# The small row transfers of a decode step's gradients: from ScalarE's queue inside wo's backward pass to SP's queue behind its last load

## The chip, the cores and the metric

The kernel runs on one core of one Trainium2 chip. The metric is device time in microseconds (us). A profiled execution has a span, which runs from its first to its last instruction, and a time, which also holds what lies around the span. The engines are named as in the profile: PE (TensorE matmuls), PEld (its weight loads), DVE (VectorE), ACT (ScalarE), POOL (GpSimd) and SP (SyncE, which here only issues transfers). PEq, ACTq and SPq are the sequencers of these engines, which issue transfers and wait on semaphores.

## What is computed

Four layers are run on one token (attention A, dense block B, A, B, with the same weights for both A and both B), and then the gradients of all weights, of both caches and of the input:

```python
def _A_ref(x, k_cache, v_cache, wq, wo):          # 32 query heads, 4 kv heads, window of 4096
    q = (x @ wq).reshape(B, Sq, Hq, Dh).transpose(0, 2, 1, 3)
    k = jnp.repeat(k_cache[:, :, Sk - W:, :], rep, axis=1)
    v = jnp.repeat(v_cache[:, :, Sk - W:, :], rep, axis=1)
    p = _softmax(jnp.einsum("bhqd,bhkd->bhqk", q, k) * (Dh ** -0.5), axis=-1)
    o = jnp.einsum("bhqk,bhkd->bhqd", p, v)
    return o.transpose(0, 2, 1, 3).reshape(B, Sq, Hq * Dh) @ wo
def _B_ref(x, w1, b1, w2):                        # mish: h * tanh(softplus(h))
    h = jnp.einsum("bsd,df->bsf", x, w1) + b1
    ...
    return jnp.einsum("bsf,fd->bsd", act, w2)
x = x + _A_ref(_layernorm(x), ...); x = x + _B_ref(_layernorm(x), ...)   # twice
_out, _vjp = jax.vjp(_f, A_x, A_k_cache, A_v_cache, A_wq, A_wo, B_w1, B_b1, B_w2)
```

With one token, the gradient of a weight matrix is a sum of two outer products, one for each use of the weight: out_4 (wq), out_5 (wo), out_6 (w1) and out_8 (w2). The caches hold 32768 positions, of which only the last 4096 have a gradient; the rest of out_2 and out_3 is written with zeros.

## The kernel before

**Weights come through a ring.** `Ring` hands out slots of 1 MB in SBUF. A load is issued on SP's queue (L71) when a slot is free; `release` frees a slot, and the next load in the list goes out when the products that read the slot are done. The last loads of the kernel are the eight chunks of wo for the backward pass of the first attention layer (key `("o", 3)`) and four chunks of wq (key `("q", 3)`, chunks 0 to 3; chunks 4 to 7 are still in the ring). They are called wo 0 to wo 7 and wq 0 to wq 3 here. A release is put off by some products (`later`), so that wq 0 goes out when wo 1 is used up, and wq 3 when wo 4 is.

**Zeros fill the memory's time.** `zeros(n)` issues n transfers of 1 MB of zeros on POOL's queue (L265). Where it is given a tile, the tile's being written holds the transfers back, so that they start at a chosen point of the calculation.

**The stage around the change** is the call of `attn_bwd(0, ...)`, from 282 us of the span on. Its first loop is wo's pass: for each of the eight chunks, PE turns blocks of 128x128 (L474) into three PSUM buffers named BIG, ACT and DVE copy them back (L309, L306), and PE multiplies them with the incoming gradient (L493); from chunk 2 on DVE takes a quarter of the chunk as a dot of rows (L451). After each chunk the function `do1` runs. Then follow the scores' gradient (L922 to L929), `dp1`, the query's gradient (L938, L940), `dq1`, and wq's pass, a loop over eight chunks with `dn1` after each.

**Rows for the gradients.** The outer products need their factors as rows, in two partitions of the tile `ROWS` (a part of W1's storage) at base 0 (out_4), 32 (out_5), 64 (out_6) and 96 (out_8). Three functions put them there by small transfers on ACT's queue:

- `rowize` turns GA, GB or DQC on PE (L1010), copies the result on ACT (L1013) and issues two transfers (L1015).
- `take_back` brings AC, NB, OC and NA back from DRAM (L819), where the forward pass had put them.
- `rowize_f` turns DHC on PE, copies it on ACT into the tile `rf` (L859) and issues two transfers (L861).

In the kernel before, `do1` calls `rowize` for GA and GB after chunk 0, `take_back` four times after chunk 1, and `rowize_f` after chunk 2. After chunk 5 it issues two transfers of zeros and sends out_0 and out_7 on ACT's queue (`store_rows`, L326; `store_f`, L871, by way of `rf` too). `dq1` calls `rowize` for DQC.

**Use of the rows.** `dp1` issues four transfers of zeros without a condition, and then calls `work(4)`: four units of outer products (L1051), which PE takes from four lists in turn. A list holds out_8 and out_6 from the start, and out_5 from `do1`'s chunk 3 on. `twins` (L1043, in `dn1` at t = 4, on SP's queue) copies all rows once more for the units after the passes, which take two matmuls side by side. From there on everything is units, their copies out of PSUM, and stores on SP's queue (L1025, L1030).

**Order of waits.** Each engine runs its instructions in the order in which the program writes them, with semaphores between engines. The transfers of SP and ACT take eight completion semaphores in turn, in program order; a transfer waits, before it is issued, for the one eight places ahead of it, whichever of the two queues that is in.

Of the kernel before, what the change touches and what calls it, by code (L numbers as in the profile page):

```python
# [15 lines left out]
P = 128  # L16
HQ = 32
# [3 lines left out]
F = 3584  # L21
G = 4
W = 4096
TD = D // P
# [69 lines left out]
def kernel(  # L94
# [22 lines left out]
    nc = tc.nc  # L117
# [13 lines left out]
    def sb(shape, dtype, name):  # L131
        return keep.tile(shape, dtype, name=name)
# [3 lines left out]
    def tmp(shape, dtype, name):  # L136

        if name not in scratch:
            scratch[name] = keep.tile(shape, dtype, name=name)
        return scratch[name]  # L140
# [31 lines left out]
    def big():  # L172
        if wide:
            wide.append(wide.pop(0))
            return wide[-1][:, 0:512]
        b = bigs[big_n[0] % len(bigs)]
        big_n[0] += 1
        return b
# [16 lines left out]
    for hi in range(4):  # L195
        r = slice(32 * hi, 32 * hi + 32)
# [4 lines left out]
    NA = sb([P, TD, 2], BF16, "NA")  # L201
    NB = sb([P, TD, 2], BF16, "NB")
    GA = sb([P, TD, 2], BF16, "GA")
    GB = sb([P, TD, 2], BF16, "GB")
    OC = sb([P, HQ, 2], BF16, "OC")
    DQC = sb([P, HQ, 2], BF16, "DQC")
    AC = sb([P, TF, 2], BF16, "AC")
# [49 lines left out]
    def zeros(n, after=None):  # L257

        if after is not None and zjobs:
            nc.gpsimd.tensor_copy(pz[0:1, pz_n[0] % 16:pz_n[0] % 16 + 1], after[0:1, 0:1])  # L260
            pz_n[0] += 1
        for _ in range(n):
            if zjobs:
                dst = zjobs.pop()
                nc.gpsimd.dma_start(dst, zt[:])  # L265
# [52 lines left out]
    def store_rows(col_bf, n, out_flat):  # L318

        b = big().bitcast(BF16)  # L320
        nc.tensor.transpose(b[0:n, 0:P], col_bf, ident_bf[:])
        k = so_n[0]
        so_n[0] += 1
        r = rt[0:n, 2 + k, :]
        nc.scalar.copy(r, b[0:n, 0:P])
        nc.scalar.dma_start(out_flat.rearrange("(t p) -> t p", p=P), r)  # L326
# [31 lines left out]
    def to_eight(bank, buf):  # L358

        nc.vector.transpose(buf[:, 0:256], bank[:, 0:256])  # L360
        return buf[:, 0:256].rearrange("p (g m) -> p g m", m=32)[:, :, 0]
# [454 lines left out]

    def take_back(name, base, off):
        r = DR[name][:].rearrange("(n l) p -> l n p", l=2)
        nc.scalar.dma_start(ROWS[base:base + 2, off:off + r.shape[1] * P].rearrange("l (n p) -> l n p", p=P), r)  # L819

    x3, st3, sA1 = attn_fwd(1, x2, st2, False, wo_hook1, last_da)
    put_by("OC", OC, HQ)
# [29 lines left out]
    def rowize_f():  # L852

        b = big().bitcast(BF16)
        for l in range(2):
            for k in range(4):
                nc.tensor.transpose(b[0:7, (4 * l + k) * P:(4 * l + k + 1) * P],
                                    DHC[:, :, l].rearrange("p (c k) -> p k c", k=4)[:, k], ident_bf[:])
        nc.scalar.copy(rf.rearrange("c (l p k) -> c l p k", l=2, k=4), b[0:7].rearrange("c (l k p) -> c l p k", l=2, k=4))  # L859
        for l in range(2):  # L860
            nc.scalar.dma_start(ROWS[64 + l:65 + l, NOFF:NOFF + F].rearrange("o (c j) -> o c j", j=512),  # L861
                              rf[:, 512 * l:512 * l + 512])

    def store_f(col):

        b = big().bitcast(BF16)
        for k in range(4):
            nc.tensor.transpose(b[0:7, k * P:(k + 1) * P], col[:].rearrange("p (c k) -> p k c", k=4)[:, k], ident_bf[:])
        r = rf[:, 0:512]
        nc.scalar.copy(r.rearrange("c (p k) -> c p k", k=4), b[0:7, 0:512].rearrange("c (k p) -> c p k", k=4))  # L870
        nc.scalar.dma_start(out_7.rearrange("(c j) -> c j", j=512), r)  # L871
# [122 lines left out]
    ROWS = W1S[:, 0:5120]  # L994
    NOFF = 1024
# [11 lines left out]
    def rowize(cols, n, base, off):  # L1007

        b = big().bitcast(BF16)
        nc.tensor.transpose(b[0:2 * n, 0:P], cols[:].rearrange("p n l -> p (n l)"), ident_bf[:])  # L1010
        k = rt_n[0]
        rt_n[0] += 1
        nc.scalar.copy(rt[0:2 * n, k, :], b[0:2 * n, 0:P])  # L1013
        for l in range(2):
            nc.scalar.dma_start(ROWS[base + l:base + l + 1, off:off + n * P].rearrange("o (t p) -> o t p", p=P),  # L1015
                              rt[l:2 * n:2, k, :])


    def store(dst, s, old, new, of, last):


        h = (of + 1) // 2
        if new == of:
            lo = sent.pop(id(s), 0)
            nc.sync.dma_start(dst[:, lo * 512:], s[:, lo * 512:of * 512])  # L1025
            stage_free.append(s)
        elif old < h <= new and wide and (last or len(firsts) < 4):
            firsts.append(0)
            sent[id(s)] = new
            nc.sync.dma_start(dst[:, 0:new * 512], s[:, 0:new * 512])  # L1030
# [14 lines left out]
    def unit_dw(base, lo, ro, dst, left):  # L1045


        b, m = rooms(left)
        for i in range(m):
            R, at = ((ROWS, base), (TWIN, base ^ 32))[i]  # L1050
            nc.tensor.matmul(b[:, 512 * i:512 * i + 512], lhsT=R[at:at + 2, lo:lo + P],  # L1051
                             rhs=R[at:at + 2, ro + 512 * i:ro + 512 * i + 512], start=True, stop=True,
                             tile_position=(at, 0))
        evac(dst[:, 0:512 * m], b[:, 0:512 * m], cost=((0.69, 0.585), (1.23, 0.95))[m - 1])
        return m

    def units_rows(base, nblk, out):

        for c in range(nblk // 4):
            s = stage_free.popleft()  # L1060
            for tt in range(4):
                n = 0
                while n < 2:
                    m = unit_dw(base, NOFF + (4 * c + tt) * P, 512 * n, s[:, tt * D + n * 512:(tt + 1) * D], 2 - n)
                    n += m
                    store(out.rearrange("(c p k) d -> p c (k d)", p=P, k=4)[:, c], s, 2 * tt + n - m, 2 * tt + n, 8,
                          c == nblk // 4 - 1)
                    yield
# [41 lines left out]
    todo = [deque() for _ in range(4)]  # L1110
# [47 lines left out]
    do1_acc = tmp([P, HQ], FP32, "da")  # L1158

    def do1(c):  # L1160
        if c == 0:
            rowize(GA, TD, 32, 0)
            rowize(GB, TD, 96, 0)
        if c == 1:
            take_back("AC", 96, NOFF)
            take_back("NB", 64, 0)
            take_back("OC", 32, NOFF)
            take_back("NA", 0, 0)
        if c == 2:
            rowize_f()  # L1170
        if c == 4:
            y = to_eight(YR, RT.rearrange("p a t s -> p (a t s)")[:, 0:512].bitcast(FP32))
            nc.vector.tensor_tensor(out=x4[:], in0=y, in1=x3[:], op=ALU.add)
        if c == 3:
            todo[1].append(units_rows(32, HQ, out_5))
        if c == 5:
            store_rows(x4[:], TD, out_0[0, 0, :])
            store_f(db)
        if c == 5:
            zeros(2, do1_acc[:, 4 * c:4 * c + 1])  # L1180

    def dp1():
        zeros(4)
# [2 lines left out]

    def dq1():
        stage_free.extendleft(KT[:, g].rearrange("p t d -> p (t d)") for g in range(G))
        rowize(DQC, HQ, 0, NOFF)
        zeros(4, DQC[:, 0, 0:1])  # L1190

# [8 lines left out]
    def units_a0(k):  # L1200
# [3 lines left out]
        work(4)  # L1204

    g0 = attn_bwd(0, sA0, g1, ("o", 3), ("q", 3), (), dict(do=do1, dp=dp1, dq=dq1, dn=dn1), units_a0)
    zeros(2, g0)
    g0b = sb([P, TD], BF16, "g0b")
# [48 lines left out]
```

## Time and profile before

| what | value |
|---|---|
| time, median of 3 runs | 456.58 us (456.39 to 457.21) |
| time of the profiled execution | 457.25 us |
| its span | 455.5 us |
| moved by the DMA engines | 181.40 MB, mean 398 GB/s |
| busy share of the span | PE 70%, DVE 58%, ACT 46%, POOL 9% |
| share of the 16 DMA engines' span | q1 (SP's queue) 65.7%, q0 (POOL's, the zeros) 31.2%, q10 (ACT's) 0.1% |

The span is split by the profile into 40 slices of 11.4 us. In its second part a digit is the busy share of a slice in tenths (9 is 90% or more); "GB/s" is what the DMA engines moved in it. A view by windows gives the same for stretches that the reader chooses, and a timeline gives instructions with start, duration, engine, line, operation and tiles, and in brackets the idle time before one and what ended it.

### The profile page before, as it was taken

The page shows a single profiled execution, that of the slowest core. Times are in us where ns is not written, and L with a number is a line of the kernel's source. Part 1 is how long each engine was busy: PE and PEld are TensorE (multiplying, and loading weights), DVE is VectorE, ACT ScalarE, POOL GpSimd, SP SyncE. Part 2 cuts the span into 40 slices and gives each one's busy share as a digit, 9 for nine tenths or more (in the row PEclk, how much of TensorE's full clock was granted, in tenths as well). Part 3 has the DMA queues.
Part 4 walks back from the last instruction along what each step waited for, and adds up shares of the span by engine and source line. Part 5 has one row for each costly group of instructions (what it writes and reads, how often), then busy time and mean ns, then how long its engine had stood idle before and what let it go on. Part 6 is the DMA issues. An engine that isn't in the chain of part 4 may idle for free. (4 is left out here: it accounts for less than half of the span.)

```text
span 455.5 us, 12838 instructions
## 1 busy us (share of the span) xinstructions
PE 318.3 (70%) x5681; PEld 244.4 (54%) x5681; DVE 262.0 (58%) x515; ACT 210.6 (46%) x245; POOL 38.9 (9%) x86
## 2 busy tenths in 40 slices
PE   3835543456699788986898567488896898889900
PEld 3735543445686688976886455487692222234500
DVE  4504746278442764763377447425476999998900
ACT  2501101011067766860384431164166999999900
POOL 1000000002132212102101000003212000000000
PEclk9955555555559899985698757858585555555555
DMA  8999999979999999999999999859999999999997
GB/s 335 422 421 419 418 420 420 419 312 425 395 422 419 422 418 414 398 417 420 424 422 423 423 417 382 328 181 371 419 392 405 408 416 419 415 420 416 406 408 298
DMA packets 28085, 181.40 MB, mean 398 GB/s; under 512 B 3674, under 2 KB 3702, under 8 KB 9462
## 3 DMA queue, kind: packets, MB, share of 16 engines
q1 hardware_dynamic: 19526, 121.76, 65.7%
q0 software_dynamic: 8064, 58.72, 31.2%
q8 instruction: 44, 0.72, 0.6%
q10 hardware_dynamic: 440, 0.10, 0.1%
q14 instruction: 11, 0.09, 0.0%
HBM read 81.84 MB, written 98.62 MB: 396 GB/s over the span
## 5 line engine op out<-in xcount | busy, mean ns | idle before, releaser
L309 ACT COPY ring<-BIG 128x1024 bf16<-128x1024 bf16 x51 | 50.5, 1014 | 56.5 <-PE BIG L474 44.5
L1051 PE MATMUL wide<-W 2*128 2x512 bf16 x228 | 52.1, 598 | 9.3 <-ACT W L309 1.9
L474 PE MATMUL BIG<-ident_bf,ring 128*128 128x128 bf16 x664 | 55.2, 237 | 3.6 <-ACT W L1013 1.6
L474 PEld LDWEIGHTS <-ring 128*128 128x128 bf16 x768 | 52.8, 109 | 5.3 <-issue 4.8
L451 DVE CUSTOM_DVE_ANT_0 junk<-ring,SC 128x1024 bf16<-128x1024 bf16 x32 | 38.9, 1216 | 10.2 <-DMA ring<-in_B_w_dram 9.8
L306 DVE COPY ring<-BIG 128x1024 bf16<-128x1024 bf16 x32 | 21.8, 690 | 28.5 <-PE BIG L474 20.8
L1051 PEld LDWEIGHTS <-W 2*128 2x128 bf16 x240 | 12.5, 102 | 43.9 <-issue 42.8
L493 PEld LDWEIGHTS <-ring 128*128 128x128 bf16 x864 | 30.5, 98 | 10.4 <-issue 6.5
L306 DVE CAST ring<-wide 128x1024 bf16<-128x1024 f32 (+1 forms) x29 | 33.8, 1201 | 3.2 <-PE wide L1051 1.4
L309 ACT CAST ring<-wide 128x1024 bf16<-128x1024 f32 (+1 forms) x35 | 32.9, 1016 | 1.3 <-PE wide L1102 0.5
L265 POOL DMA_DIRECT2D out_dram<-zt x56 | 29.7, 534 | 40.8 <-DMA out_dram<-zt 39.7
L309 ACT COPY KT<-BIG 128x1024 bf16<-128x1024 bf16 x22 | 21.8, 1008 | 21.8 <-PE BIG L652 19.9
L451 DVE CUSTOM_DVE_ANT_0 junk<-ring,DSX 128x1024 bf16<-128x1024 bf16 x24 | 29.4, 1225 | 0.8
L474 PE MATMUL BIG<-ident_bf,W 128*128 128x128 bf16 x288 | 25.7, 243 | 2.0 <-issue 1.7
L309 ACT COPY W<-BIG 128x1024 bf16<-128x1024 bf16 x21 | 20.8, 1014 | 9.1 <-PE BIG L474 8.6
L536 PE MATMUL MV<-NA,ring 128*128 128x1 bf16 x512 | 15.3, 165 | 13.3 <-DMA ring<-in_A_wq_dram 11.9
L536 PEld LDWEIGHTS <-ring 128*128 128x128 bf16 x512 | 14.6, 103 | 14.1 <-DMA ring<-in_A_wq_dram 12.6
L306 DVE CAST VS<-wide 128x1024 bf16<-128x1024 f32 (+1 forms) x17 | 19.7, 1188 | 3.6 <-PE wide L1051 3.0
L1102 PE MATMUL wide<-W 32*128 32x256 bf16 x128 | 20.9, 402 | 0.9 <-ACT ring L309 0.8
L474 PEld LDWEIGHTS <-W 128*128 128x128 bf16 x288 | 20.3, 117 | 2.2 <-issue 2.1
L309 ACT CAST KT<-wide 128x1024 bf16<-128x1024 f32 x20 | 20.4, 1030 | 1.8 <-PE wide L1051 0.9
L347 PE MATMUL YR<-ring,AC 128*32 128x256 bf16 x208 | 10.9, 368 | 11.0 <-DMA ring<-in_B_w_dram 8.6
(272 smaller groups left out, 522.7 us busy)
## 6 DMA issues: line engine op xcount, KB each, us to landing
out_dram<-zt POOLq DMA_DIRECT2D x56, 1024.0 KB, 20.1
ring<-in_A_wq_dram SPq DMA_DIRECT2D x24, 1024.0 KB, 12.4
ring<-in_A_wo_dram SPq DMA_DIRECT2D x14, 1024.0 KB, 14.9
ring<-in_B_w_dram SPq DMA_DIRECT2D x13, 1024.0 KB, 17.8
W<-in_A_wo_dram SPq DMA_DIRECT2D x10, 1024.0 KB, 19.8
W<-in_B_w_dram SPq DMA_DIRECT2D x8, 896.0 KB, 17.7
out_dram<-ring SPq DMA_DIRECT2D x7, 1024.0 KB
out_dram<-ring SPq DMA_DIRECT2D x13, 512.0 KB, 13.9
```

The source lines that it names most:

```text
L265: nc.gpsimd.dma_start(dst, zt[:])
L306: nc.vector.tensor_copy(dst, src)
L309: nc.scalar.copy(dst, src)
L347: nc.tensor.matmul(bank[32 * j:32 * j + 32, 0:n].rearrange("p (g a) -> p g a", a=m.shape[-1]), lhsT=vec.to_broadcast([P, 32]), rhs=m, star ...
L451: nc.vector.tensor_tensor_reduce(out=out, in0=a, in1=vec, scale=1.0, scalar=acc if i else 0.0, op0=ALU.mult, op1=ALU.add, accum_out=acc)
L474: nc.tensor.transpose(b[:, i * P:(i + 1) * P], block(w, i) if block else w[:, i * P:(i + 1) * P], ident_bf[:])
L493: nc.tensor.matmul(out, lhsT=w[:, i * P:(i + 1) * P], rhs=rhs_of(i), start=fresh[0], stop=last and i == n - 1, skip_group_check=True)
L536: nc.tensor.matmul(q_ps[:, h:h + 1], lhsT=ch[:, h * P:(h + 1) * P], rhs=NA[:, t, l:l + 1], start=(k == 0 and h == 0), stop=(k == TD - 1), ...
L1051: nc.tensor.matmul(b[:, 512 * i:512 * i + 512], lhsT=R[at:at + 2, lo:lo + P], rhs=R[at:at + 2, ro + 512 * i:ro + 512 * i + 512], start=Tru ...
L1102: nc.tensor.matmul(b[:, k * 256:(k + 1) * 256], lhsT=RT[32 * g:32 * g + 32, a, tp, :], rhs=YS[32 * g:32 * g + 32, :], start=True, stop=Tru ...
```

## The change

`do1` no longer makes rows after chunks 0, 1 and 2. After chunk 5 it brings back AC, OC, NB and NA, and after chunk 6 it makes the rows of GA, GB and DHC. All row transfers of the three functions, those of DQC in `dq1` too, are issued on SP's queue. The list of out_5 starts in `dq1`, so that the four units in `dp1` come from out_6 and out_8 alone. `store_f` now uses `rf` ahead of `rowize_f`. The `twins`, the zeros, the loads and the units are as before.

```diff
     def take_back(name, base, off):
         r = DR[name][:].rearrange("(n l) p -> l n p", l=2)
-        nc.scalar.dma_start(ROWS[base:base + 2, off:off + r.shape[1] * P].rearrange("l (n p) -> l n p", p=P), r)
+        nc.sync.dma_start(ROWS[base:base + 2, off:off + r.shape[1] * P].rearrange("l (n p) -> l n p", p=P), r)
...
         for l in range(2):
-            nc.scalar.dma_start(ROWS[64 + l:65 + l, NOFF:NOFF + F].rearrange("o (c j) -> o c j", j=512),
+            nc.sync.dma_start(ROWS[64 + l:65 + l, NOFF:NOFF + F].rearrange("o (c j) -> o c j", j=512),
                               rf[:, 512 * l:512 * l + 512])
...
         for l in range(2):
-            nc.scalar.dma_start(ROWS[base + l:base + l + 1, off:off + n * P].rearrange("o (t p) -> o t p", p=P),
+            nc.sync.dma_start(ROWS[base + l:base + l + 1, off:off + n * P].rearrange("o (t p) -> o t p", p=P),
                               rt[l:2 * n:2, k, :])
...
     def do1(c):
-        if c == 0:
-            rowize(GA, TD, 32, 0)
-            rowize(GB, TD, 96, 0)
-        if c == 1:
-            take_back("AC", 96, NOFF)
-            take_back("NB", 64, 0)
-            take_back("OC", 32, NOFF)
-            take_back("NA", 0, 0)
-        if c == 2:
-            rowize_f()
         if c == 4:
             y = to_eight(YR, RT.rearrange("p a t s -> p (a t s)")[:, 0:512].bitcast(FP32))
             nc.vector.tensor_tensor(out=x4[:], in0=y, in1=x3[:], op=ALU.add)
-        if c == 3:
-            todo[1].append(units_rows(32, HQ, out_5))
         if c == 5:
             store_rows(x4[:], TD, out_0[0, 0, :])
             store_f(db)
+            zeros(2, do1_acc[:, 4 * c:4 * c + 1])
+        if c == 6:
+            rowize(GA, TD, 32, 0)
+            rowize(GB, TD, 96, 0)
+            rowize_f()
         if c == 5:
-            zeros(2, do1_acc[:, 4 * c:4 * c + 1])
+            take_back("AC", 96, NOFF)
+            take_back("OC", 32, NOFF)
+            take_back("NB", 64, 0)
+            take_back("NA", 0, 0)
...
     def dq1():
         stage_free.extendleft(KT[:, g].rearrange("p t d -> p (t d)") for g in range(G))
+        todo[1].append(units_rows(32, HQ, out_5))
         rowize(DQC, HQ, 0, NOFF)
```

## The prediction

> **What bounds the kernel now.** I read the page first: its second part, by slices.
>
> ```profile
> span 455.5 us, 12838 instructions
> DMA  8999999979999999999999999859999999999997
> GB/s 335 422 421 419 418 420 420 419 312 425 395 422 419 422 418 414 398 417 420 424 422 423 423 417 382 328 181 371 419 392 405 408 416 419 415 420 416 406 408 298
> ```
>
> The DMA engines are at 90% or more in nearly every slice: the kernel is bound by the memory, and an end that comes earlier needs time in which these engines now stand still. The deepest gap after the start is slice 27 (296 to 307 us, digit 5, 181 GB/s), inside wo's last pass. Next the windows of 1 us there. The columns are the window, busy us (instructions) of PE, PEld, DVE, ACT and POOL, the granted clock, the DMA share and GB/s.
>
> ```profile
> 293.00:294.00 1.00, 0.00 (x0) 0.00 (x0) 0.00 (x0) 0.00 (x0) 0.00 (x0) 0.50 0.65 256
> 294.00:295.00 1.00, 0.00 (x0) 0.00 (x0) 0.00 (x0) 0.00 (x0) 0.00 (x0) 0.50 0.23 90
> 296.00:297.00 1.00, 0.00 (x0) 0.00 (x0) 0.00 (x0) 0.39 (x1) 0.00 (x0) 0.50 0.08 33
> 299.00:300.00 1.00, 1.00 (x25) 1.00 (x23) 0.00 (x0) 0.72 (x1) 0.00 (x0) 0.50 0.00 0
> 301.00:302.00 1.00, 1.00 (x20) 1.00 (x18) 0.00 (x0) 0.64 (x1) 0.00 (x0) 0.50 0.90 131
> 339.00:340.00 1.00, 1.00 (x38) 0.91 (x35) 0.94 (x2) 0.42 (x1) 0.96 (x2) 1.00 0.49 197
> ```
>
> The missing shares from 293 to 302 sum to 7.3 us of the mean engine. At 339 there is a second, short gap (0.15 at 338 and 0.51 at 339, 0.7 us together). The timeline of ACT and of SP says who makes the first:
>
> ```profile
> 288.52 1.01 ACT L309 COPY ring<-BIG 128x1024 bf16<-128x1024 bf16 x1 [1.37 <-PE BIG L474]
> 291.32 0.26 ACTq L819 DMA_DIRECT2D W<-dr_AC  x1
> 293.82 0.25 ACTq L819 DMA_DIRECT2D W<-dr_NB  x1
> 296.29 0.23 ACTq L819 DMA_DIRECT2D W<-dr_NA  x1
> 296.61 1.93 ACT L309 COPY ring<-BIG 128x1024 bf16<-128x1024 bf16 x2 [7.08 <-DMA W<-in_A_wo_dram]
> ...
> 300.12 0.33 SPq L71 DMA_DIRECT2D ring<-in_A_wq_dram  x1
> 303.70 0.33 SPq L71 DMA_DIRECT2D ring<-in_A_wq_dram  x1
> 306.05 0.33 SPq L71 DMA_DIRECT2D ring<-in_A_wq_dram  x1
> 307.54 0.33 SPq L71 DMA_DIRECT2D W<-in_A_wq_dram  x1
> ```
>
> ACT copies nothing for 7.08 us, because each of its row transfers waits for a load of wo eight places ahead in the turn of semaphores. The landing events of the trace put wo 4, 5 and 6 at 291.30, 293.80 and 296.26; the issues of AC, NB and NA follow each within 0.03 us. Meanwhile both free BIG buffers are full, PE stands, no chunk is released, and wq 0 goes out only at 300.12. This pattern (a row transfer waits for a whole load) is what I carry to the new place.
>
> **What the change removes.** ACT loses, inside the pass, four L1015 issues (1.79 + 1.29 us), four L819 (0.26 + 0.25 + 0.28 + 0.23), two L861 (1.51) and the 7.08 us of waiting. The dots of DVE give the pass's own step: chunk 2 at 289.10, chunk 3 at 291.48 (2.38 apart), chunk 4 at 302.71 (11.23). So the stall costs the pass 11.23 - 2.38 = 8.85 us. Its end (L903, at 314.61) would come near 306. Chunks 5 to 7 can't be turned before they land (293.80, 296.26, 298.72), which fits that. The loads wq 0 to 3 then go out from about 289.5 to 296 (each 2.4 us after the other, from wo 0's release, which the trace shows at 289.55 and which frees wo 7). The gap at 293 to 302 is filled: 7.3 us for the mean engine, less for the last one (wo 7's last share lands at 289.55 + 9.2 = 298.7; wq 0's data, 2.5 us of a load that lands at 305.3, can't have started before 302).
>
> **What it moves.** Copies of 0.25, 0.26 and 1.00 us go to chunk 6 of the pass. The last, into `rf`, now follows out_7's transfer, which reads `rf`: it was under way for 6.5 us (issue 309.59, landing event 316.05), so ACT and, with all three BIG buffers taken by the three turns, PE can stand at chunk 7 for up to about 5 us. I cost that at nothing, because the units behind it wait longer, as follows; without that cover it would be those 5 us of pass.
>
> SP's order is now: wq 3, AC, OC, NB, NA, GA, GA, GB, GB, F, F (the rows of DHC), DQC, DQC, twins, stores. In the turn of eight, AC follows wo 6, OC wo 7, NB wq 0, NA out_0, GA wq 1 and out_7, GB wq 2 and wq 3, and F follows AC and OC. So the second GB can't be issued before all of wq 3 has landed, and F stands behind it. The four units in `dp1` (L1051) take F, NB, GB and AC, and PE's order puts them ahead of the query's gradient. Behind them wait L938, DVE's L940, ACT's copy of DQC, the zeros of `dq1` and wq's pass.
>
> ```profile
> 320.08 0.61 PE L1051 MATMUL BIG<-W 2*128 2x512 bf16 x3
> 326.05 0.20 DVE L940 TENSOR_SCALAR DQC<-MV 128x32 bf16<-128x32 f32 x1 [3.25 <-PE MV L938]
> 326.55 2.10 POOL L265 DMA_DIRECT2D out_dram<-zt  x4
> 339.04 1.05 POOL L265 DMA_DIRECT2D out_dram<-zt  x2
> ```
>
> *When wq 3 lands.* 1 MB (1.049e6 bytes) at 420 GB/s (window 285 to 290) takes 2.5 us. The slowest DMA engine ends wo 7 at 298.7. Four loads follow: 308.7. The two zeros of chunk 5 go out near 295.5 and share the engines: in the trace wq 3 beside zeros needs 9.3 us to land (307.54 to the event at 316.86), wq 1 without them 4.7. That adds 2 x 2.5: 313.7. `dp1`'s four zeros come after the pass, from about 309.5 to 312, and take half of what is left of wq 3: 1 to 4 us more. Bounds 313.7 and 317.5; I take 315.5.
>
> *When F has landed.* Issues of GB (1.29 / 2) and F (1.51 / 2) are 1.4 us. Landing of small rows: at most 7.3 us (L1015's DQC beside zeros), at least 4.7 (a load that is alone); the first rows of L1015, at 285 to 288 beside loads, took 4.9 to 5.9 by their events. I take 5.6. F: 315.5 + 1.4 + 5.6 = 322.5, bounds 313.7 + 1.4 + 4.7 = 319.8 and 317.5 + 1.4 + 7.3 = 326.2.
>
> *What is late then.* The units start at 322.5 and not at 320.08: +2.4 us (bounds -0.3 and +6.1). The zeros of `dq1` move from 326.55 to 329. The DMA engines have, after wo 7 (most done by 294, the last at 298.7), four loads and six zeros: 10 x 2.5 = 25 us, to 319 (most) and 323.7 (last). They stand until about 331, where new data flows some 2 us after the issue. So the gap comes back, 7 to 12 us long, at 319 to 331. From 329 on the order is as before: 12.5 us (326.55 to 339.04) to the zeros of `dn1`, whose ahead-lying 4 x 2.5 = 10 us run out first, as at 339 now. The end therefore moves with the units of `dp1`. Taken off: ACT no longer issues DQC's rows (327.91, 2.06 us); its next copy waited for PE, so I take 0.4 us, bounds 0 and 1.0.
>
> *Not on the path:* the twins (now all behind DQC's rows, used after 348; SP's first store is at 350.28); out_5's later start (the same units in another order, where the DMA share is 1.01 to 1.02 from 350 to 450); three copies on ACT, which stands.
>
> **Sum.** +2.4 - 0.4 = +2.0 us. The span goes from 455.5 to 457.5, the execution around it from 457.25 to 459.25; against the median of 456.58, which lies 0.7 under the profiled time, 458.6. From the bounds: -0.3 - 1.0 and +6.1, that is 455.3 to 462.7.
>
> **Rivals.** (1) *The rows come in time and the gap is gone*: wq 3 lands by 309 because the zeros take less of the share, and F by 315, near the time at which PE gets to the units (pass end 306 to 308 plus 5.5, the distance from 314.61 to 320.08). For it: the loads do start 10 us earlier. Against it: two zeros are surely issued among them. The gain is bound by the last engine's idle time, 302 - 298.7 = 3.3, plus 1.1 before wq 1, and at most the mean's 7.3; I take 4.5: 452.1. It decides once F lands before 318. The Trainium skill, in "DMA: Bandwidth & Descriptors", section "Issuing engines are not separate DMA queues", says that transfers of all issuing engines interleave on the same 16 DMA engines, so that the issuer matters for its sequencer's time alone; by that, moving the rows off ACT is all gain, which is this rival. The trace has the other half: at 293.82 and 296.29 it was the wait before the issue that cost time.
>
> (2) *No change*: F lands between 319.6 and 321.4, the lower end of my bounds; the gap is moved whole, 456.6.
>
> (3) *Much slower*: rows crawl beside the zeros (7.3 us and more), `dp1`'s zeros take their full half, and F lands after 325: +4.9 to +7 us, 462.6. For it: DQC's 7.3 us. Against: the earlier rows' 4.9 to 5.9.
>
> That the change doesn't do what it says I leave out: as built, all row transfers stand behind wq 3 on SP.
>
> **Chances.** Forecast (+0.9 to +4.9) 0.40, rival 1 0.22, rival 2 0.18, rival 3 0.20. Under 0.2% (0.9 us) no change can be told. Faster 0.22, within 0.18, slower 0.60. The range reaches from rival 1's price to above rival 3's, 452.5 to 464; the forecast's own is 457.5 to 461.5.
>
> **What would show it.** Right: L819 and L1015 on SP, the second GB just after wq 3's landing at 314 to 317; no ACT wait above 2 us before chunk 6; wq 0 issued by 292; PE standing some 8 us before L1051, released by a transfer W<-W; a DMA gap at 319 to 331 in place of 293 to 302. Wrong: L1051 in `dp1` before 318, the gap gone, or a pass that isn't shorter (the `rf` wait more than 5 us).

## The result, and the profile after

The changed kernel takes 458.37 us (median of 10 runs, 457.28 to 459.48) against 456.58 (10 runs, 456.12 to 458.46). The ratio is 1.0033, 95% interval 1.0018 to 1.0048: slower by 1.8 us (0.3%, small but outside the noise), where 2.0 were forecast. The profiled execution is one of the shorter ones (457.36 us, span 455.6). First its page, by slices:

```profile
span 455.6 us, 12833 instructions
DMA  8999999989999999999999999998399999999998
GB/s 335 419 423 420 416 420 420 418 316 422 391 426 420 423 421 414 400 420 422 425 416 423 424 393 365 422 418 359 129 368 404 412 410 420 415 422 419 404 409 324
```

Slice 27, which had a digit of 5 and 181 GB/s, is full now (418 GB/s). The hole is two slices further on: digit 3 and 129 GB/s in slice 29. The windows of 1 us of the changed kernel (window, busy us of PE, PEld, DVE, ACT, POOL, granted clock, DMA share, GB/s) give its edges:

```profile
309.00:310.00 1.00, 0.46 (x11) 0.37 (x11) 0.59 (x4) 0.00 (x0) 0.18 (x1) 0.50 0.57 214
310.00:311.00 1.00, 1.00 (x44) 1.00 (x42) 0.00 (x0) 0.00 (x0) 0.98 (x3) 0.50 0.25 84
...
321.00:322.00 1.00, 0.00 (x0) 0.00 (x0) 0.00 (x0) 0.00 (x0) 0.00 (x0) 0.50 0.47 187
326.00:327.00 1.00, 1.00 (x44) 1.00 (x42) 0.00 (x0) 0.00 (x0) 0.00 (x0) 0.50 0.00 0
...
340.00:341.00 1.00, 1.00 (x37) 0.91 (x34) 1.00 (x2) 0.30 (x1) 0.98 (x2) 1.00 0.31 119
```

From 321 to 330 the missing shares sum to 7.7 us of the mean engine, at 308 to 311 to 1.2, at 339 to 341 to 1.0: 9.9 us in place of the 7.3 + 0.7 before. The difference of 1.9 us lies near the 1.8 us of the medians. That is no proof of a price, because the experiments show below that time isn't lost at the rate of the mean engine's idle time. The timeline of the changed kernel shows who holds whom:

```profile
291.10 3.94 SPq L71 DMA_DIRECT2D ring<-in_A_wq_dram  x3
296.20 0.33 SPq L71 DMA_DIRECT2D W<-in_A_wq_dram  x1
...
305.14 1.00 ACT L859 COPY W<-BIG 7x1024 bf16<-7x1024 bf16 x1 [4.05 <-DMA out_dram<-W]
...
310.06 2.10 POOL L265 DMA_DIRECT2D out_dram<-zt  x4
...
314.05 0.64 SPq L1015 DMA_DIRECT2D W<-W  x1
314.79 2.69 SPq L861 DMA_DIRECT2D W<-W  x2
...
322.43 1.01 PE L1051 MATMUL BIG<-W 2*128 2x512 bf16 x3 [8.55 <-DMA W<-W]
...
328.31 2.10 POOL L265 DMA_DIRECT2D out_dram<-zt  x4
339.93 1.05 POOL L265 DMA_DIRECT2D out_dram<-zt  x2
```

The loads wq 0 to 3 go out 9 to 11 us earlier than before. The landing events of the trace, 16 for a transfer of 1 MB, tell when each DMA engine's share of it is there. 14 shares of wq 3 are there by 310.21, the 15th at 311.60 and the last at 314.04; the second GB row is issued at 314.05, 0.01 us later. So for its last 2.4 us the row waits for one engine's share alone. The second row of DHC lands at 322.30, and PE, which has stood for 8.55 us, starts `dp1`'s units at 322.43.

### The profile page after: what moved, and what is told of

It is laid out like the page before. It is cut to its first block, busy times and chain, and to the rows that moved or that the text cites. A ratio compares the mean times of both kernels' runs of the same rounds, so it can differ in the third digit from the quotient of the medians.

```text
span 455.6 us, 12833 instructions
## 1 busy us (share of the span) xinstructions
PE 317.9 (70%) x5681; PEld 244.5 (54%) x5681; DVE 261.9 (57%) x516; ACT 210.6 (46%) x244; POOL 38.9 (9%) x86
## 5 line engine op out<-in xcount | busy, mean ns | idle before, releaser
L474 PE MATMUL BIG<-ident_bf,ring 128*128 128x128 bf16 x664 | 56.3, 242 | 4.4 <-ACT W L859 3.6
L474 PEld LDWEIGHTS <-ring 128*128 128x128 bf16 x768 | 54.6, 111 | 5.6 <-issue 5.1
L1051 PE MATMUL wide<-W 2*128 2x512 bf16 x228 | 50.3, 598 | 9.5 <-DVE KT L306 1.7
L493 PEld LDWEIGHTS <-ring 128*128 128x128 bf16 x864 | 30.1, 98 | 12.4 <-issue 6.1
L306 DVE CAST ring<-wide 128x1024 bf16<-128x1024 f32 (+1 forms) x28 | 32.6, 1199 | 3.1 <-PE wide L1102 1.0
L474 PE MATMUL BIG<-ident_bf,W 128*128 128x128 bf16 x288 | 23.5, 228 | 0.4 <-issue 0.3
L306 DVE CAST KT<-wide 128x1024 bf16<-128x1024 f32 (+1 forms) x17 | 20.1, 1188 | 3.8 <-PE wide L1051 2.8
L536 PEld LDWEIGHTS <-ring 128*128 128x128 bf16 x512 | 14.6, 103 | 13.9 <-DMA ring<-in_A_wq_dram 12.4
L309 ACT CAST VS<-wide 128x1024 bf16<-128x1024 f32 (+1 forms) x20 | 19.4, 1010 | 1.1 <-PE wide L1051 0.6
L474 PEld LDWEIGHTS <-W 128*128 128x128 bf16 x288 | 18.5, 112 | 0.7 <-issue 0.4
```

Of the source, the lines that this page charges most:

```text
L306: nc.vector.tensor_copy(dst, src)
L309: nc.scalar.copy(dst, src)
L474: nc.tensor.transpose(b[:, i * P:(i + 1) * P], block(w, i) if block else w[:, i * P:(i + 1) * P], ident_bf[:])
L493: nc.tensor.matmul(out, lhsT=w[:, i * P:(i + 1) * P], rhs=rhs_of(i), start=fresh[0], stop=last and i == n - 1, skip_group_check=True)
L536: nc.tensor.matmul(q_ps[:, h:h + 1], lhsT=ch[:, h * P:(h + 1) * P], rhs=NA[:, t, l:l + 1], start=(k == 0 and h == 0), stop=(k == TD - 1), ...
```

## The experiments

All times are medians; a ratio is to the kernel before, measured beside it (456.7 to 457.0 us).

### The units of dp1 later

```diff
 def dp1():
     zeros(4)
     stage_free.extendleft(VS[:, g].rearrange("p t d -> p (t d)") for g in range(G))
-    work(4)
```

> The changed kernel without the four units of outer products in dp1 (they come with the units after the passes). Theory (PE stands before these units until the rows of DHC have landed, and the zeros of dq1 stand behind them): PE goes from the scores' gradient to the query's at about 315, the zeros of dq1 are issued near 320 and not at 328, the DMA gap at 321 to 329 is gone, 450 to 454 us. Rival (the end is set by something else, the wait for the rows only fills time that was free): 457.5 to 459.5 us with the gap at another place.

450.47 us, ratio 0.9869 (0.9854 to 0.9883), from one line less in the changed kernel. Its timeline:

```profile
312.40 3.56 PE L938 MATMUL MV<-DSX,KT 128*128 128x8 bf16 x128
...
316.49 2.10 POOL L265 DMA_DIRECT2D out_dram<-zt  x4
329.33 1.05 POOL L265 DMA_DIRECT2D out_dram<-zt  x2
```

One of its windows, at the place of the changed kernel's hole:

```profile
326.00:327.00 1.00, 1.00 (x27) 1.00 (x25) 0.88 (x2) 1.00 (x2) 0.00 (x0) 1.00 1.00 371
```

The query's gradient starts at 312.40 and not behind the rows (second row of DHC: 323.89), the zeros of `dq1` 11.8 us earlier than in the changed kernel. No window from 310 to 330 has a DMA share under 0.9. So it is PE's order, in which the units stand ahead of the query's gradient, that turns late rows into an idle memory. The rows themselves are as late as ever and nobody needs them yet. That it is the wait before the units and not their work is shown by two runs below: with the rows on POOL's queue, where the units don't wait, the kernel takes 452.63 us with them in `dp1` and 452.49 without.

### All rows on POOL's queue, in the old places

```diff
-        nc.scalar.dma_start(ROWS[base:base + 2, ...
+        nc.gpsimd.dma_start(ROWS[base:base + 2, ...
...
-            nc.scalar.dma_start(ROWS[64 + l:65 + l, ...
+            nc.gpsimd.dma_start(ROWS[64 + l:65 + l, ...
...
-            nc.scalar.dma_start(ROWS[base + l:base + l + 1, ...
+            nc.gpsimd.dma_start(ROWS[base + l:base + l + 1, ...
```

> The kernel before with all row transfers on POOL's queue, in their old places after chunks 0, 1 and 2, so that neither ACT nor SP waits for the loads eight places ahead. Theory (in both kernels it is the wait for whole loads, in ACT's order or in front of the rows, that makes the gap): no ACT wait in the pass, wq 0 issued by 292, rows of DHC landed by 303, units of dp1 at about 308 without a wait, no DMA gap from 293 to 330, 449 to 453 us. Rival (POOL's issues are slow or its rows crawl beside the loads): units of dp1 not before 316, 455 us or more.

452.63 us, ratio 0.9913 (0.9899 to 0.9928). In the trace POOL's transfers take eight semaphores of their own in turn. The earlier users there are zeros or other rows and no load of weights, and they have landed or are about to: the longest such wait is that of NA, issued at 289.93 behind zeros that land at 289.65. The pass does not stand behind it, since neither ACT nor SP issues a row. The timeline, and two windows at the places of the two holes:

```profile
291.92 1.22 POOL L861 DMA_DIRECT2D W<-W  x2 [1.43 <-ACT W L859]
...
308.70 0.61 PE L1051 MATMUL BIG<-W 2*128 2x512 bf16 x3
```

```profile
298.00:299.00 1.00, 1.00 (x23) 1.00 (x24) 0.95 (x1) 0.58 (x2) 0.38 (x1) 1.00 1.00 418
326.00:327.00 1.00, 1.00 (x32) 1.00 (x29) 1.00 (x2) 1.00 (x2) 0.00 (x0) 1.00 1.02 426
```

The rows of DHC are issued from 291.92 on, have landed by 298.48, and the units start at 308.70 with no wait before them. Both holes are gone. The kernel is still 2.2 us slower than the one without the units in `dp1`; two runs below follow that up.

### The new places on ACT's queue

```diff
-        nc.sync.dma_start(ROWS[base:base + 2, ...        # and the two others
+        nc.scalar.dma_start(ROWS[base:base + 2, ...
```

> The changed kernel with its rows on ACT's queue again, in the new places (after chunks 5 and 6). Theory (the wait for the load eight places ahead counts, and it goes with the transfer to whatever engine issues it): ACT stands in chunks 5 to 7 until wq 3 has landed at about 314, the pass ends near 319, the gap is 311 to 322, 459 to 463 us. Rival (the rows are late because they stand behind 1 MB loads in SP's own queue): on ACT's queue they land by 306, 451 to 456 us.

458.70 us, ratio 1.0043 (1.0026 to 1.0059), 0.3 us under what was expected. ACT's timeline in chunks 6 and 7:

```profile
302.29 0.23 ACTq L819 DMA_DIRECT2D W<-dr_NB  x1
304.04 0.23 ACTq L819 DMA_DIRECT2D W<-dr_NA  x1
304.39 1.93 ACT L309 COPY W<-BIG 128x1024 bf16<-128x1024 bf16 x2 [5.41 <-DMA W<-in_A_wq_dram]
...
314.07 1.52 ACTq L861 DMA_DIRECT2D W<-W  x2
```

The landing events put wq 0 at 302.26, out_0 at 304.02 and wq 3 at 313.99; NB, NA and the rows of DHC are issued within 0.1 us of them, on another queue than SP's. The rows of DHC land at 317.21, 5 us earlier than on SP's queue, with little else under way (DMA shares of 0.00 to 0.11 from 314 to 318), but now the pass itself ends late: `dp1`'s zeros go out at 319.67, the units at 323.42. The hole from 307 to 321 is 11.8 us of the mean engine. The wait belongs to the transfer's place in the turn of eight and goes with it to either of these two queues; on ACT the pass pays, on SP the rows' users pay.

### out_7 behind the rows of DHC

```diff
             store_rows(x4[:], TD, out_0[0, 0, :])
-            store_f(db)
             zeros(2, do1_acc[:, 4 * c:4 * c + 1])
...
             rowize_f()
+        if c == 7:
+            store_f(db)
```

> The changed kernel with out_7's transfer after chunk 7, so that the copy of DHC's rows does not wait for it (4.05 us of ACT in the profile of the changed kernel). Theory (that wait has a cover, the rows wait for wq 3 anyway): the pass ends some 4 us earlier, dp1's zeros start at about 306 and take a share from wq 2 and wq 3, which land 1 to 3 us later, and the units of dp1 too: 458 to 461.5 us. Rival (the wait costs what it shows): 453.5 to 455.5 us.

459.34 us, ratio 1.0056 (1.0041 to 1.0071), 1.0 us above the changed kernel by the medians; the two intervals overlap, so what is sure is that nothing was gained. Its timeline of POOL:

```profile
305.77 2.11 POOL L265 DMA_DIRECT2D out_dram<-zt  x4
330.52 2.10 POOL L265 DMA_DIRECT2D out_dram<-zt  x4
341.79 1.05 POOL L265 DMA_DIRECT2D out_dram<-zt  x2
```

Without ACT's wait of 4.05 us `dp1`'s zeros start 4.3 us earlier, and wq 3, which shares the engines with them, lands at 317.53 and not at 314.04. The second row of DHC goes out later still, at 320.66, since OC, eight places ahead of it, lands at 320.64 beside those zeros. The units start at 324.65 (322.43), `dn1`'s zeros 1.9 us later. So that wait on `rf` was free in the changed kernel, and by this trace it kept zeros out of the way of a load and a row that all waited for.

### The old places on SP's queue

```diff
-        nc.scalar.dma_start(ROWS[base:base + 2, ...        # kernel before; and the two others
+        nc.sync.dma_start(ROWS[base:base + 2, ...
```

> The kernel before with its row transfers on SP's queue in their old places (after chunks 0, 1 and 2), so ahead of wo 7 and of wq 0 to 3. Theory (the wait for a load eight places ahead goes with the rows to SP; there it holds back loads, and the last DMA engine's idle time is what counts): wo 7 goes out only behind NA's wait for wo 6 (about 296.5 us) and wq 0 behind it; ACT does not stand; the rows of DHC land by 305 and dp1's units don't wait. The last engine idles some 2 us in place of 4.4: 453 to 455.5 us. Rival (loads held back on SP cost as much as ACT's stall did): 456 to 458 us.

454.77 us, ratio 0.9959 (0.9946 to 0.9971). The timeline of SP:

```profile
295.91 0.22 SPq L819 DMA_DIRECT2D W<-dr_OC  x1
296.18 0.32 SPq L819 DMA_DIRECT2D W<-dr_NA  x1
296.61 0.36 SPq L71 DMA_DIRECT2D ring<-in_A_wo_dram  x1
```

wo 7 stands behind OC, which waits for wo 6 (landed at 295.89), and behind NA, and goes out 7 us later than before. The DMA engines idle in part from 290 to 297 (shares between 0.01 and 0.74) and at 298 (0.53). But the rows are there early (second row of DHC at 303.75), the units start at 315.28 without a wait, and no other hole follows. A surprise is wq 0 at 303.62: in the turn it now follows out_0 on ACT, which lands at 303.55, though the zeros of chunk 5 fill that time.

### The 4.05 us wait, with the units late

```diff
-        r = rf[:, 0:512]                        # in store_f, on top of the kernel without units in dp1
+        r = RT.rearrange("p a t s -> p (a t s)")[0:7, 1024:1536]
```

> e1_units_late with a buffer of its own for out_7, so that ACT's copy of DHC's rows doesn't wait for out_7 and dp1's zeros start some 3.5 us earlier. That fills the gap which e1_units_late still has at 307 to 310 us (1.2 us of the mean engine; the last DMA engine is busy then). Theory (the last DMA engine sets the end): 450.0 to 451.0 us, the same as e1_units_late's 450.47. Rival (the mean engine's idle time counts): 449.0 to 449.6 us.

450.91 us, ratio 0.9880 (0.9861 to 0.9900): nothing gained, although the hole at 307 to 310 is gone (no window under 0.8 from 288 to 350).

### POOL's queue, with the units late

```diff
 def dp1():
     zeros(4)
     stage_free.extendleft(VS[:, g].rearrange("p t d -> p (t d)") for g in range(G))
-    work(4)                                     # in the kernel with all rows on POOL's queue
```

> e2_rows_on_pool without the four units in dp1. e2_rows_on_pool has no DMA gap and is still 2.2 us slower than e1_units_late; its last DMA engine ends 6.2 us behind the others, e1_units_late's 2 us behind the next. Theory (the rows on POOL's queue leave more work on the last engine, or take it later): 452 to 453.5 us. Rival (the four units before the query's gradient cost the 2.2 us): 450 to 451 us.

452.49 us, ratio 0.9908 (0.9888 to 0.9929): the units were not what made the rows on POOL's queue 2.2 us worse. The windows at the end of three kernels, the one before, the one with rows on POOL's queue (second experiment), and the sixth experiment's:

```profile
448.00:452.00 4.00, 0.00 (x0) 0.00 (x0) 0.00 (x0) 0.00 (x0) 0.00 (x0) 0.50 1.01 401
```

```profile
444.00:448.00 4.00, 0.00 (x0) 0.00 (x0) 0.00 (x0) 0.00 (x0) 0.00 (x0) 0.50 0.07 27
448.00:452.00 4.00, 0.00 (x0) 0.00 (x0) 0.00 (x0) 0.00 (x0) 0.00 (x0) 0.50 0.02 7
```

```profile
444.00:448.00 4.00, 0.00 (x0) 0.00 (x0) 0.00 (x0) 0.00 (x0) 0.00 (x0) 0.50 0.06 24
```

A share of 0.06 is one engine of 16. In the kernel before all engines work to the end. With rows on POOL's queue 15 engines finish by 443.4 and one at 449.6; in the sixth 14 by 441.9, one at 443.1 and one at 448.0. The holes that the experiments filled were idle time of the other engines first: in these runs the end is set by one late engine, which had little of it to give. Why it ends 1.7 us later with the rows on POOL's queue (449.6) than without the units in `dp1` (447.9, first experiment) stays open.

### Splitting late stores

```diff
-            nc.sync.dma_start(dst[:, lo * 512:], s[:, lo * 512:of * 512])
+            if last and of == 8 and lo == 4 and len(parted) < 4:      # four stores, on top of the sixth experiment
+                parted.append(0)
+                nc.sync.dma_start(dst[0:120, lo * 512:], s[0:120, lo * 512:of * 512])
+                nc.sync.dma_start(dst[120:128, lo * 512:], s[120:128, lo * 512:of * 512])
+            else:
+                nc.sync.dma_start(dst[:, lo * 512:], s[:, lo * 512:of * 512])
```

> e6_units_late_rf_free with four of the late half-chunk stores (0.5 MB) issued as 120 partitions and 8 partitions. In e6_units_late_rf_free 14 of 16 DMA engines end by 441.9, the last at 448.0, by the landing events of its last store. Theory (one engine has more to do and sets the end; the Trainium skill, in DMA: Bandwidth & Descriptors, section Why a DMA increments its semaphore by 16 and not by 1, states that a transfer of 120 partitions would run on the 15 lowest engines; if the late one is the sixteenth, each split store spares it 32 KB, some 1.25 us at 26 GB/s): the last store lands by 444.5, 446 to 448 us. Rival (the late engine is one of the lower ones, which get 1/15 and the 8 partitions more): 451 to 452.5 us. If the end is set by all engines together: 450.5 to 451.5 us.

453.52 us, ratio 0.9922 (0.9906 to 0.9938): slower than any of the three cases. The late engine takes part in the transfers of 120 partitions (one of 15 shares lands at 429.2, the others by 424.5) and in those of 8 (429.4, the others by 424.7): it was not the one that was to be spared. The four extra transfers also take places in the turn of eight, in which each store waits for the late engine's share of an older one (the two parts of one of them go out at 418.40 and 420.60, right behind last shares at 418.33 and 420.58), and the other engines ran dry meanwhile:

```profile
420.00:425.00 5.00, 1.01 (x7) 0.39 (x3) 2.28 (x2) 1.51 (x2) 0.00 (x0) 0.50 0.63 184
425.00:430.00 5.00, 0.00 (x0) 0.00 (x0) 0.00 (x0) 0.00 (x0) 0.00 (x0) 0.50 0.68 218
```

That this is the whole of the 2.6 us is not shown, and what makes that engine late stays open.

### The changed kernel again

> The changed kernel once more, for a second profile: its ten times go from 457.28 to 459.48 us, and its profile is one of the shortest (457.36). The same chain is expected (wq 3 landed at 313 to 318, units of dp1 8 us after the rows' issue, zeros of dq1 near 328 to 331, a gap of 7 to 9 us before them), 457.3 to 459.5 us. If times vary with the moment at which wq 3 lands, a longer run has it later.

458.18 us, ratio 1.0027 (1.0009 to 1.0045). This profiled execution took 459.0 us (span 457.2) and not 457.36:

```profile
316.17 0.63 SPq L1015 DMA_DIRECT2D W<-W  x1
...
323.82 1.01 PE L1051 MATMUL BIG<-W 2*128 2x512 bf16 x3 [10.51 <-DMA W<-W]
...
341.15 1.05 POOL L265 DMA_DIRECT2D out_dram<-zt  x2
```

wq 3 lands at 316.15 and not at 314.04, and what follows is late too: units +1.4 us, `dn1`'s zeros +1.2, the span +1.6. But some of this comes from ahead of the stage. DVE's cast of GA, with which the stage begins, in the kernel before, the changed one and this run:

```profile
282.37 0.17 DVE L889 CAST GA<-g_B 128x8 bf16<-128x8 f32 x1
```

```profile
283.35 0.17 DVE L889 CAST GA<-g_B 128x8 bf16<-128x8 f32 x1
```

```profile
284.54 0.17 DVE L889 CAST GA<-g_B 128x8 bf16<-128x8 f32 x1
```

Over the eleven profiles it lies between 279.85 and 284.54, although no experiment changes what comes before it. A difference of a microsecond or two between the times of two traces is therefore not the change's alone. wo 7's last share lands only 0.7 us later here (299.59 and 298.93); and `dp1`'s zeros go out 0.6 us earlier (309.49 and 310.06), ahead of wq 3's last share. That they took its place in the late engine fits, but two executions don't prove it.

## Why the prediction was right

The forecast was the likeliest case, and its chain held link by link, with one term mis-sized; the numbers are for the two profiles of the changed kernel, 457.36 and 459.0 us.

- *The bound, and the hole's maker.* Taking ACT out of the waits filled slice 27 as said. The 7.3 us that were read there belong to 293 to 306; the windows from 293 to 302 sum to 6.7. That the place in the turn is to blame, and whoever stands behind it, is shown by the rows on POOL's queue (nothing late behind them, no hole, 452.63) and on ACT's in the new places (same waits, 458.70).
- *The pass* was expected to end near 306, up to 5 us later with the wait on `rf`; it ends at 308.7 and 308.1 (L903) against 314.7 before.
- *wq 3's landing*, taken at 315.5 (313.7 to 317.5): 314.04 and 316.15.
- *DHC's rows*, taken at 322.5: 322.30 and 323.69. The landing took 6.2 and 5.4 us (5.6 taken). From the issue of GB's second row to that of DHC's second it took 2.1 us, for 1.4.
- *The cover of ACT's wait on `rf`* (up to 5 us, costed at nothing): 4.05 us. The fourth experiment bears the cover out: without the wait the kernel is no faster, and 1.0 us slower by the medians.
- *The zeros of `dq1`*, at 329: 328.31 and 329.70. *The gap at 319 to 331*: 321 to 330. The small hole at 308 to 311, 1.2 us, I had not seen: `dp1`'s zeros come after the four loads and two zeros are through on most engines.
- *The way from the units to `dn1`'s zeros* was shorter than I took it: 17.5 and 17.3 us in place of 19.0 before, where I took off 0.4. Of that, 0.6 lies between the units and `dq1`'s zeros: L938 runs in one piece of 3.58 us, where before it took 4.14 in two. Another 0.9 to 1.0 lies behind them, the whole of my bound for ACT's spared issues. `dn1`'s zeros are late by 0.9 and 2.1 us, against 2.0.
- *The end*: +0.1 and +1.7 us by the spans, +1.8 by the medians. The last engine has done `dq1`'s zeros at 342.30 and 344.20 (341.99 before), which is +0.3 and +2.2.

So the mechanism was right, and that the sum came within 0.3 us of the median is in part luck. The way was 1.1 to 1.2 us shorter than taken; the units were later than taken by 1.3 us in the one profile, which made up for it, and not in the other, whose span grew by 0.1 us.

The last engine's idle time is the better measure, and it can be read from the last shares of consecutive 1 MB transfers, which follow each other by 2.5 us where transfers stand in line. Before, the step from wo 7 to wq 0 is 6.54 us and the next 3.09: 4.6 us too long (3.3 + 1.1 taken). In the changed kernel the step from `dp1`'s last zeros to `dq1`'s first is 9.64 and 10.31 us: 7.1 and 7.8 too long. With the new places on ACT's queue (median 458.70) it is 8.8 us, with out_7 behind the rows of DHC (459.34) 9.0, and with the old places on SP's queue (454.77) 3.2, at wo 7. In the four kernels at 450.47 to 452.63 us no hole of this kind is left. The order of the medians is that of the excess; the amounts agree only roughly, and each is read in one or two executions.

The rivals: the faster one (452.1) was refuted as a forecast, since the rows landed after 318. But its condition and its price were right: where the units don't wait, on POOL's queue, the time is 452.63, a gain near the last engine's idle time of 4.4 to 4.6 us and not the mean's. Of the Trainium skill's rule that the issuer matters for its sequencer's time alone ("DMA: Bandwidth & Descriptors", section "Issuing engines are not separate DMA queues"), the runs show the limit: the same rows from three queues gave 452.63 (POOL), 454.77 (SP) and 456.58 us (ACT), all in the old places, and what differed was which transfer a row waits for before its issue and who stands behind it.

The best version here beats both kernels: the changed one without the units in `dp1`, 450.47 us, 1.3% under the kernel before.

## What to carry to other kernels

A small transfer can inherit the wait of a 1 MB load through the completion semaphore that both take in turn; so before it is moved to another queue, count which transfer stands so many places ahead of it, and who stands behind it. A stall that is taken out of one engine's order comes back where the result is needed: look for the first instruction that uses it and ask whether that can be moved back too, which here was worth 7.9 us and was one line. Where the memory is the bound, look for the DMA engine that finishes last: in these runs its idle time could be turned into time, and the mean engine's could not beyond it.

## What the hardware showed that was not expected

One share of 16 ends behind the others: by 1.2 us in the kernel before (454.6 against 453.3 for the next), 6.2 with the rows on POOL's queue, 4.9 in the sixth experiment, and only 0.1 and 0.7 in the two profiles of the changed kernel. The records don't name the engine; that it is one and the same is taken from its even steps. The holes in the kernel before hid it, because it could catch up there while the other engines stood. That filling a hole of 7.3 us of the mean engine gave some 4 us (456.58 to 452.63 and 452.49) to 6 us (450.47) and not more fits this. The late engine also lengthens the waits that this case is about: a row behind a load waits for that load's last share, which comes 2.4 us (wq 3 in the changed kernel) to 4.1 us (in its second profile) behind the 15th.

Whether a difference early on reaches the end depends on what waits for it. The second profile of the changed kernel began the stage 1.2 us later than the first, and its span is 1.6 us longer; the sixth experiment's profile began it 2.6 us earlier than the first experiment's (279.92 and 282.56), and their spans are the same (448.9 and 448.8).
